# Reciprocal root-mean-square of four head pairs on GpSimd instead of ScalarE, in a fused attention and feed-forward kernel

## Chip, cores and metric

One core of a Trainium2 chip runs the whole kernel. The metric is the device time of one execution in microseconds, given as the median of several runs. A core has a matrix engine (TensorE, PE in the profile), a vector engine (VectorE, DVE), an engine for activation functions (ScalarE, ACT), a general engine (GpSimd, POOL) and a queue that only starts transfers (SyncE, SP). Each engine takes its own instructions strictly in the order in which the program gives them, and waits on semaphores for the results of the others.

## What is computed

The inputs are `q`, `k`, `v` of shape (8, 12, 448, 64): 8 batches, 12 heads, 448 positions, 64 values for each. Cut to what matters:

```python
def rmsnorm(x, g):
    rms = np.sqrt(np.mean(x * x, axis=-1, keepdims=True) + 1e-06)
    return x / rms * g

q_n, k_n = rmsnorm(q, g_q), rmsnorm(k, g_k)
scores = q_n @ k_n.T / sqrt(64)                 # for each batch and head
attn = softmax(scores)
x = (attn @ v).transpose(0, 2, 1, 3).reshape(3584, 768)
out = gelu_tanh(x @ w_in) @ w_out               # w_in 768x2048, w_out 2048x768
```

The change touches only `1 / rms` of the first batch.

## The kernel before

The 12 heads of a batch are worked on as 6 pairs, 0 to 5; a pair fills the 128 partitions with two heads of 64 values. Two pairs make a chunk `c` (pairs 0 and 1, 2 and 3, 4 and 5), and `j` tells which pair of the chunk it is. For batches 1 to 7 the normalization of a batch is done while an earlier batch is in its matrix products. Batch 0 has nothing ahead of it, so its normalization, scores, softmax and products with `v` are woven by hand into a list of steps, `FRONT` (L761 to L774). The function `front` (L669) turns one word of that list into instructions. The order of the words is the order in which each engine gets its work, and nothing reorders it.

The words that matter here, with the pair's number behind them; the letter behind a colon is the engine (A for ScalarE, D for VectorE, P for GpSimd):

- `sq4:P`, `sk4:P`: squares of `q` or `k` of pair 4 (L186 on ScalarE, L188 elsewhere).
- `tq4`, `tk4`: VectorE sums the 64 squares (L203) into `ssq`, 8 columns for `q` and 6 or 8 for `k`.
- `rs4`: `rsqrt` (L205) makes `1 / rms` of both `q` and `k` of the pair, 14 columns for an even pair and 16 for an odd one. ScalarE does it as `Ln` of `ssq / 64 + 1e-6` (L209) and `Exp` of minus one half of that (L212), into the tile `rinv`.
- `nq4:P`, `nk4:P`: `raw * rinv`, to bf16 (L226), on the engine named.
- `tpq4`, `tpk4`: TensorE transposes the result (L238, L245); `cq4`, `ck4`: VectorE copies it from PSUM (L255, L264).
- `s14`: TensorE's scores of one tile of 128 keys for two heads (L324, L310), in one of two PSUM places; `e14`: ScalarE's exponential of that tile (L331), after which the place is free again. There are 21 tiles, seven for each chunk.
- `sa`, `sb`, `xa`, `xb`: the products of a pair with ones, for the sums, and with `v` (L370); `st`, `rc`, `rb`, `xt`: VectorE's reciprocals of the sums, and the scaled result `xT` (L377 to L395).
- `w0` to `w3`, `o0` to `o3`: GpSimd starts the loads of the weights (L630, L636); `v0` to `v2` those of `v`.
- `mb`, `ma`, `mc`, `md`, `g`: the first matrix product of the feed-forward part (L412) and its GELU (L421).

The part of the list around the change:

```
sq0:A sk0:P gcol tq0 tk0 sq1:P rs0 sk1:A nq0:P v1 nk0:D shift tq1 tk1 sq2:A tpq0 tpk0 v2
v0 sk2:A rs1 sq3:A cq0:D ck0:D tq2 s0 e0 y3 s1 nk1:D nq1:D L11 e1 tpk1 tpq1 s2 sk3:P w0
tq3 tk2 rs2 e2 ck1:D cq1:D s3 e3 sa0 s4 sk4:P tk3 nq2:D nk2:D rs3 tpk2 tpq2 s5 sb0 tk4
ck2:D cq2:D nq3:D st0 e4 nk3:P e5 s6 sk5:P L12 e6 tpk3 tpq3 s7 e7 s8 sa1 s9 sb1 xa0 e8
sq4:P sq5:P w1 rc0 cq3:D rb0 ck3:D tq4 tk5 rs4 e9 xb0 s10 st1 xt0 rc1 rb1 tq5 e10 sa2
s11 e11 rs5 nk4:P nq4:P w2 nk5:P nq5:P xa1 xb1 sb2 s12 e12 s13 tpk4 tpq4 xt1 st2 ck4:D
cq4:D rc2 xa2 e13 rb2 sa3 xb2 s14 tpk5 tpq5 s15 e14 xt2 ck5:D cq5:D sb3 e15 U s16 s17
```

Read for one engine, the list gives its queue. GpSimd's from `sk3` on is: `sk3`, `w0`, `sk4`, `nk3`, `sk5`, `sq4`, `sq5`, `w1`, `nk4`, `nq4`, `w2`, `nk5`, `nq5`, `w3`, `o0`, then squares of the next batch.

Of the kernel before, what the change touches and what calls it, by code (L numbers as in the profile page):

```python
# [8 lines left out]
F32 = mybir.dt.float32  # L9
BF16 = mybir.dt.bfloat16  # L10
AF = mybir.ActivationFunctionType  # L11
ALU = mybir.AluOpType  # L12
# [4 lines left out]
def kernel(  # L17
# [11 lines left out]
    nc = tc.nc  # L29
    B, H, S, D = q.shape  # L30
# [19 lines left out]
    consts = ctx.enter_context(tc.tile_pool(name="consts", bufs=1))  # L50
# [11 lines left out]
    op = ctx.enter_context(tc.tile_pool(name="op", bufs=3))  # L62
# [37 lines left out]
    kT = consts.tile([128, NCH, NS, 128], BF16)  # L100

    NU = 4 * CH + 2 * NS
    ssq = [consts.tile([128, NCH, NU], F32, name=f"ss{i}") for i in range(3)]
    raws, sqs, rinvs, nrms = {}, {}, {}, {}
    qT, xT = {}, {}
# [98 lines left out]

    def rsqrt(b, c=slice(0, NCH), at=slice(0, NU)):  # L205
        if b not in rinvs:
            rinvs[b] = smp.tile([128, NCH, NU], F32, tag="rinv", name="rinv")
        lg = smp.tile([128, NCH, NU], F32, tag="lg", name="lg")
        nc.scalar.activation(  # L209
            lg[:, c, at], ssq[b % 3][:, c, at], AF.Ln, scale=1.0 / D, bias=eps  # L210
        )
        nc.scalar.activation(rinvs[b][:, c, at], lg[:, c, at], AF.Exp, scale=-0.5)  # L212
# [397 lines left out]
    nc.vector.memset(ones, 1.0)  # L610
    nc.vector.memset(rows, 1.0)
    nc.vector.memset(ssq[0], 1.0)
    nc.gpsimd.memset(onesr, 0.0)
    for j in range(2):
        nc.gpsimd.memset(onesr[own(j), j], 1.0)
# [53 lines left out]
    def front(step):  # L669
# [7 lines left out]
        elif name in ("tq", "tk"):  # L677
            total(0, c, n, j)
        elif name == "rS":
            rsqrt(0, i, slice(0, 30))  # L680
        elif name == "rs":
            rsqrt(0, c, slice(14 * j, 14 + 16 * j))
        elif name in ("nq", "nk"):
            normed(0, c, n, j, eng)
# [46 lines left out]
        elif name == "o":  # L731
            w_out_part(i // 2, slice(i % 2 * nf // 2, (i % 2 + 1) * nf // 2))
        elif name == "L":
            loads(*divmod(i, 10))
        elif name in ("Sq", "Sk"):
            square(1, i, n, eng)
        elif name in ("Tq", "Tk"):
            total(1, i, n)
        elif name == "Rs":
            rsqrt(1, slice(0, 2))  # L740
        elif name in ("Nq", "Nk"):
            normed(1, i // 10, n, i % 10, eng)
        elif name == "Tp":
            tps["Q", i] = trans(1, i, "q", ps_o, "o")
            tps["K", i] = trans(1, i, "k", ps_m, "mm")
        elif name in ("Cq", "Ck"):
            (place_q if n == "q" else place_k)(1, i, tps[n.upper(), i], eng)
        elif name in ("GELU", "EXP"):
            nc.scalar.preload_act_table_set(EXP_SET if name == "EXP" else GELU_SET)
        elif name == "mb":  # L750
            mm1(0, [0, 1], [i], act=False)
        elif name in ("ma", "mc", "md"):
            fs = [2 * i, 2 * i + 1] if i < 7 else [i + 7]
            cs = {"ma": range(4), "mc": [4], "md": [5] if i < 3 else range(HP)}[name]
            mm1(0, fs, cs, act=False)
        elif name == "g":
            gelu(0, [2 * i, 2 * i + 1] if i < 7 else [i + 7])
        else:
            raise ValueError(step)
# [176 lines left out]
```

## Time and profile before

| | |
|---|---|
| time, median of 3 runs | 413.02 us (412.62 to 413.85) |
| the profiled execution: its time | 413.83 us |
| its span from first to last instruction | 412.1 us |
| busy in the span: TensorE | 403.7 us (98%) |
| VectorE | 274.3 us (67%) |
| ScalarE | 296.2 us (72%) |
| GpSimd | 131.8 us (32%) |

The profile is one execution. All its times count from the start of the span. A row of the timeline gives the start, the duration, the engine, the line, the operation and its tiles; a bracket behind it gives how long the engine had been idle and what ended that. Neighbours of one line are put together with their count. Transposes have the line 238 or 245, and which pair they belong to follows from the order of the list. A row for a stretch gives the busy time of each engine in it and the granted clock of TensorE as a share of full speed. Ends of matrix instructions are modelled, so that busy does not mean working at full rate.

### The profile page before, as it was taken

What the parts mean: (1) busy time and instruction counts of PE and PEld (TensorE: products, weight loads), DVE (VectorE), ACT (ScalarE), POOL (GpSimd) and SP (SyncE); (2) the same over time, 40 slices, a digit from 0 to 9 for tenths busy, and PEclk for the clock granted to TensorE, in tenths of its full rate; (3) what the DMA queues carried; (4) which work ended last, traced back from release to release, by engine and by line L of the source; (5) the groups of instructions that cost most, each with busy time, mean ns of one, the idle gap of its engine ahead of it and who ended that gap; (6) DMA issues with size and microseconds to landing.
All of it is one profiled execution on the core that took longest, in us unless ns stands there. A gap on an engine that the chain in (4) does not pass through costs nothing.

```text
span 412.1 us, 10085 instructions
## 1 busy us (share of the span) xinstructions
PE 403.7 (98%) x4207; PEld 243.5 (59%) x4207; DVE 274.3 (67%) x454; ACT 296.2 (72%) x398; POOL 131.8 (32%) x144
## 2 busy tenths in 40 slices
PE   8799999999999999999999999999999999999996
PEld 3344555566655666557655666556655575556664
DVE  4899739899899638884678747786488633783010
ACT  5797987969988587767977778785976558774300
POOL 7689000234500942037500745019310460000000
PEclk9699999999999999999999999999999999999999
DMA  8999995999981689229981399616991161210022
GB/s 191 227 235 228 203 196 141 227 227 192 213 145 38 139 176 207 66 52 176 222 140 41 78 203 171 136 40 145 171 145 40 23 112 40 72 46 2 2 77 78
DMA packets 97870, 54.21 MB, mean 132 GB/s; under 512 B 63776, under 2 KB 94368, under 8 KB 97824
## 3 DMA queue, kind: packets, MB, share of 16 engines
q1 hardware_dynamic: 71392, 41.69, 43.4%
q0 software_dynamic: 26112, 11.80, 22.5%
q8 instruction: 33, 0.54, 0.6%
q10 hardware_dynamic: 320, 0.07, 0.1%
q14 instruction: 13, 0.11, 0.1%
HBM read 45.61 MB, written 11.01 MB: 137 GB/s over the span
## 4 chain that ended last, share of the span: by engine, by line
PE 95%; SPq 2%; DMA 1%; DVE 0%; ACT 0%; issue 0%; ACTq 0%; DVEq 0%
PE o L441 36%; PE hh L412 31%; PE o L370 11%; PE sc L324 8%; PE h L412 5%; PE sc L310 1%; DMA rawq<-in_q_dram 1%; PE ox L370 1%; SPq L143 1%; SPq L118 1%; SPq L136 1%; PE tp L245 0%; PE o L477 0%; PE tp L238 0%; ACT ex L331 0%
## 5 line engine op out<-in xcount | busy, mean ns | idle before, releaser
L441 PE MATMUL o<-wout,g 128*64 128x384 bf16 (+1 forms) x1648 | 160.6, 327 | 0.0
L331 ACT ACTIVATE ex<-sc,shift 128x896 bf16<-128x896 f32 x144 | 136.1, 1011 | 1.3 <-PE sc L324 1.3
L412 PE MATMUL hh<-xT,win 128*64 128x448 bf16 (+1 forms) x1260 | 133.8, 353 | 0.0
L441 PEld LDWEIGHTS <-g 128*64 128x64 bf16 (+1 forms) x1648 | 96.2, 109 | 58.3 <-issue 14.8
L412 PEld LDWEIGHTS <-win 128*64 128x64 bf16 (+1 forms) x1440 | 95.4, 109 | 49.9 <-issue 3.2
L421 ACT ACTIVATE g<-hh 128x896 bf16<-128x896 f32 x56 | 50.1, 919 | 44.5 <-PE hh L412 44.4
L203 DVE TENSOR_REDUCE ss<-sq 128x14 f32<-128x896 f32 (+4 forms) x45 | 47.9, 1080 | 32.4 <-ACT sq L186 19.9
L454 ACT COPY osb<-o 128x384 f32<-128x384 f32 x50 | 24.2, 483 | 47.8 <-PE o L441 47.8
L788 POOL COPY mark<-es 1x1 bf16<-1x1 bf16 x8 | 1.8, 225 | 162.9 <-DVE es L345 158.5
L377 DVE STREAM_TRANSPOSE st<-o 128x448 f32<-128x448 f32 x48 | 31.1, 648 | 23.6 <-PE o L370 23.2
L324 PE MATMUL sc<-qT,kT 64*128 64x448 bf16 (+1 forms) x372 | 39.6, 360 | 1.7 <-DVE kT L264 1.3
L345 DVE TENSOR_TENSOR es<-ex 128x896 bf16<-128x896 bf16 x42 | 26.8, 637 | 12.0 <-ACT ex L331 12.0
L226 POOL TENSOR_TENSOR nrmq<-rawq,rinv 112x512 bf16<-112x512 f32 x33 | 34.0, 1043 | 0.0
L226 POOL TENSOR_TENSOR nrmk<-rawk,rinv 128x512 bf16<-128x512 f32 (+1 forms) x33 | 31.1, 957 | 4.2 <-ACT rinv L212 4.2
L385 DVE STREAM_TRANSPOSE rb<-rc 128x448 f32<-128x448 f32 x48 | 31.0, 645 | 1.6
L370 PE MATMUL o<-ex,vb 128*64 128x448 bf16 x252 | 30.9, 352 | 0.0
L279 DVE TENSOR_SCALAR kT<-kT,gcol 128x896 bf16<-128x896 bf16 x19 | 21.1, 1108 | 11.7 <-DMA kT<-nrmk 11.7
L343 DVE TENSOR_TENSOR es<-es,exr 64x896 bf16<-64x896 bf16 x42 | 25.9, 617 | 2.4 <-ACT exr L331 1.0
L345 DVE TENSOR_TENSOR es<-es,ex 128x896 bf16<-128x896 bf16 x42 | 25.5, 608 | 2.3 <-ACT ex L331 0.3
L395 DVE TENSOR_TENSOR xT<-o,rb 128x448 bf16<-128x448 f32 x42 | 25.8, 615 | 1.4 <-PE o L370 0.9
L188 POOL TENSOR_TENSOR sq<-rawq 112x1024 f32<-112x1024 f32 x9 | 17.0, 1893 | 28.4 <-DMA rawq<-in_q_dram 25.0
L324 PEld LDWEIGHTS <-kT 64*128 64x128 bf16 (+1 forms) x372 | 10.9, 99 | 24.6 <-issue 18.1
(83 smaller groups left out, 349.4 us busy)
## 6 DMA issues: line engine op xcount, KB each, us to landing
rawq<-in_q_dram SPq DMA_DIRECT2D x48, 224.0 KB, 4.4
rawk<-in_k_dram SPq DMA_DIRECT2D x48, 192.0 KB, 4.6
vb<-in_v_dram POOLq DMA_DIRECT2D x8, 576.0 KB, 10.1
win<-in_moe_w_in_dram POOLq DMA_DIRECT2D x4, 768.0 KB, 14.1
wout<-in_moe_w_out_dram POOLq DMA_DIRECT2D x4, 768.0 KB, 20.4
out_dram<-osb SPq DMA_DIRECT2D x7, 336.0 KB, 4.3
out_dram<-osb SPq DMA_DIRECT2D x8, 288.0 KB, 2.7
out_dram<-osb SPq DMA_DIRECT2D x8, 240.0 KB, 2.6
```

The lines of the kernel that those rows point to most:

```text
L203: nc.vector.reduce_sum(stat(ssq[b % 3], b, c, n, j), view(n, sqs[n, b, c], j), axis=AX.X)
L226: eng.tensor_mul(dst.rearrange("p t a d -> p a t d"), view(n, raws[n, b, c], j), r.to_broadcast(list(r.shape) + [D]),)
L324: nc.tensor.matmul(sc[o, a, :S], kT[r, c, 4 * j + t, o], qT[b][r, hp], start=True, stop=True,)
L331: nc.scalar.activation(dst, sc[:, :, :S], AF.Exp, scale=scale, bias=shift)
L343: nc.vector.tensor_add(es[p], es[p], exrs[b, hp // 2][p])
L345: nc.vector.tensor_add(es, ex[:, 0] if t == 1 else es, ex[:, t])
L370: nc.tensor.matmul(o[a * D:(a + 1) * D], w(a), e[:, a], start=(i == 0), stop=(i + 1 == len(steps)),)
L377: nc.vector.transpose(oas["st"].rearrange("p a b -> p (a b)"), oas[0])
L385: nc.vector.transpose(oas["rb", hp], oas["rc"].to_broadcast([128, S // 32, 32]))
L412: nc.tensor.matmul(h[i * m:(i + 1) * m, j, :S], win[:, c // 2 + NCH * (c % 2), f * 128 + i * m:f * 128 + (i + 1) * m], xT[b][:, c], start= ...
L421: nc.scalar.activation(g[:, fs[0]:fs[0] + len(fs), (b % 2) * S:(b % 2 + 1) * S], hs1[fs[0]][:, :, :S], AF.Gelu_apprx_tanh)
L441: nc.tensor.matmul(o[j * m:(j + 1) * m, :HD], g[:, f, i * 128 + j * m:i * 128 + (j + 1) * m], wout[:, f, half * HD:(half + 1) * HD], start ...
```

## The change

For batch 0 and the chunks 1 and 2, that is in `rs2`, `rs3`, `rs4` and `rs5`, `rsqrt` issues two GpSimd instructions in place of the two ScalarE ones: `ssq / 64 + 1e-6` into `rinv`, then `rinv` to the power of `half`, a constant tile that holds minus one half, in place. `rs0`, `rs1` and all later batches stay on ScalarE. The constant is written by one GpSimd instruction at the start of the program. The list of steps is not changed, so the new instructions stand in GpSimd's queue where the words `rs2` to `rs5` stand in the list: `sk3`, `w0`, `rs2`, `sk4`, `rs3`, `nk3`, `sk5`, `sq4`, `sq5`, `w1`, `rs4`, `rs5`, `nk4`, `nq4`, `w2`, `nk5`, `nq5`.

```diff
     NU = 4 * CH + 2 * NS
+    half = consts.tile([128, NU], F32)
     ssq = [consts.tile([128, NCH, NU], F32, name=f"ss{i}") for i in range(3)]
...
         lg = smp.tile([128, NCH, NU], F32, tag="lg", name="lg")
+        if b == 0 and c > 0:
+            r_ = rinvs[b][:, c, at]
+            nc.gpsimd.tensor_scalar(
+                r_, ssq[b % 3][:, c, at], 1.0 / D, 1e-6, op0=ALU.mult, op1=ALU.add)
+            nc.gpsimd.tensor_tensor(r_, r_, half[:, at], op=ALU.pow)
+            return
         nc.scalar.activation(
             lg[:, c, at], ssq[b % 3][:, c, at], AF.Ln, scale=1.0 / D, bias=eps
         )
...
     nc.vector.memset(ssq[0], 1.0)
+    nc.gpsimd.memset(half, -0.5)
     nc.gpsimd.memset(onesr, 0.0)
```

## The prediction

> **What bounds the kernel now.** I read the span first, then the busy time by stretch, then the chain of waits through the stretch of the change, and last the queues of single engines.
>
> ```profile
> span 412.1 us, 10085 instructions
> ```
>
> The profiled execution took 413.83 us, so 1.7 us lie around its span; it stands 0.81 us above the median of 413.02. I work out a shift D of the end on the rows of this execution and add it to the median.
>
> ```profile
> 10.00:20.00 10.00, 7.31 (x46) 2.85 (x47) 9.21 (x19) 7.82 (x14) 6.43 (x7) 0.70 1.35 227
> 20.00:30.00 10.00, 9.59 (x92) 4.54 (x90) 9.16 (x20) 9.33 (x14) 8.62 (x10) 0.96 1.18 237
> 30.00:36.00 6.00, 6.00 (x50) 2.75 (x51) 5.61 (x10) 5.98 (x7) 5.97 (x5) 1.00 1.19 233
> ```
>
> The columns are the stretch, its length, the busy time of TensorE, its weight loads, VectorE, ScalarE and GpSimd, TensorE's clock, and the transfers. The first batch is the only place where TensorE is not always at work: 2.69 us idle from 10 to 20, 0.41 us from 20 to 30, none from 30 to 36. ScalarE is as full as TensorE from 20 to 36, which makes it tempting to free it.
>
> ```profile
> 13.82 0.53 DVE ss L203
> ...
> 21.09 1.02 ACT ex L331
> 22.10 0.04 issue
> 22.14 0.36 PE sc L324 x2
> ...
> 37.27 0.86 PE hh L412 x4
> ```
>
> This is the chain of waits between 8 and 38 us, 57 pieces. Up to 14.8 it runs through transfers and VectorE, and from there through TensorE, with one visit to ScalarE. Behind 22.14 every piece is TensorE's own. So whatever holds TensorE for a microsecond after 22 us moves the end by a microsecond, unless it saves it elsewhere. What ScalarE costs TensorE in the whole kernel is one row of the waits:
>
> ```profile
> PE sc L324 <- ACT ex L331: 0.4, 1, 0.4
> ```
>
> **What is removed.** Eight ScalarE instructions, four of each kind.
>
> ```profile
> L209 ACT ACTIVATE lg<-ss,eps x7: 292/307/344, 6.0 to 42.3; 128x14 f32<-128x14 f32 x3, 128x16 f32<-128x16 f32 x3, 128x60 f32<-128x60 f32 x1
> L212 ACT ACTIVATE rinv<-lg x7: 214/217/252, 6.4 to 42.7; 128x14 f32<-128x14 f32 x3, 128x16 f32<-128x16 f32 x3, 128x60 f32<-128x60 f32 x1
> ```
>
> By the medians, in ns, that is 4 x (0.307 + 0.217) = 2.1 us of ScalarE. On the path it is worth at most the 0.41 us above.
>
> **What is added.** The constant's write lies in the first 4 us, while GpSimd waits for data: nothing. Each of `rs2` to `rs5` is now two small GpSimd instructions. No row shows a power on GpSimd; the nearest are its multiplications, whose last column is the mean in ns:
>
> ```profile
> L188 POOL TENSOR_TENSOR sq<-rawq 112x1024 f32<-112x1024 f32 x9 | 17.0, 1893 | 28.4 <-DMA rawq<-in_q_dram 25.0 <-DVE ss L203 3.4
> ...
> L188 POOL TENSOR_TENSOR g<-rawk 128x384 f32<-128x384 f32 x2 | 1.7, 834 | 1.0 <-DMA rawk<-in_k_dram 1.0
> ```
>
> The slope is (1893 - 834) / 640 = 1.65 ns a column and the fixed part 0.20 us, so 16 columns multiplied cost 0.22 us. I take that for the first instruction. The power costs at least as much, 0.22 us, and I put its upper end at the longest of these rows, 1.89 us; between them I take the geometric mean, 0.65 us, an estimate, since a power is several multiplications' work on few columns and the fixed part does not grow. With 0.05 us between the two, one `rs` takes 0.92 us (0.49 to 2.16), against 0.55 us on ScalarE.
>
> The Trainium skill ("GPSIMD Engine Reference", section 2.1) says that the first call to a freshly loaded GpSimd kernel pays about 6 us for loading code; if the power were such a call, `rs2` would end 5 us later and I estimate about 421.5. The first multiplications here show nothing of that kind (the 0.84 us of the row at 13.62 below), so the sum leaves it out.
>
> **What is moved.** The order of GpSimd's queue, which is what costs:
>
> ```profile
> 13.62 0.84 POOL L188 TENSOR_TENSOR g<-rawk 128x384 f32<-128x384 f32 x1
> ...
> 23.52 0.82 POOL L226 TENSOR_TENSOR nrmk<-rawk,rinv 128x384 bf16<-128x384 f32 x1 [0.90 <-ACT rinv L212]
> 24.31 1.03 POOL L226 TENSOR_TENSOR nrmq<-rawq,rinv 112x512 bf16<-112x512 f32 x1
> 25.30 0.88 POOL L630 DMA_DIRECT2D win<-in_moe_w_in_dram  x1
> 26.66 1.04 POOL L226 TENSOR_TENSOR nrmk<-rawk,rinv 128x512 bf16<-128x512 f32 x1 [0.47 <-ACT rinv L212]
> 27.66 1.03 POOL L226 TENSOR_TENSOR nrmq<-rawq,rinv 112x512 bf16<-112x512 f32 x1
> ```
>
> These are `sk4`, then `nk4`, `nq4`, `w2`, `nk5`, `nq5`. On ScalarE, `rs5` waited for VectorE's `tq5` and nothing of pair 4 stood behind it. On GpSimd `nk4` and `nq4` do: the list has `rs4`, `rs5`, `nk4`, `nq4`. VectorE's rows:
>
> ```profile
> 11.78 1.53 DVE L226 TENSOR_TENSOR nrmq<-rawq,rinv 112x512 bf16<-112x512 f32 x1
> ...
> 15.57 0.67 DVE L226 TENSOR_TENSOR nrmq<-rawq,rinv 112x512 bf16<-112x512 f32 x1
> 16.17 0.54 DVE L226 TENSOR_TENSOR nrmk<-rawk,rinv 128x384 bf16<-128x384 f32 x1
> ...
> 25.18 0.64 DVE L203 TENSOR_REDUCE ss<-g 112x8 f32<-112x512 f32 x1
> ```
>
> They are `nq1`, `nq2`, `nk2` and `tq5`, which ends at 25.82. And who waits for the normalized pairs, on TensorE:
>
> ```profile
> 16.99 0.50 PE L245 MATMUL tp<-ident,nrmk 128*128 128x128 bf16 x3
> ...
> 26.55 0.34 PE L245 MATMUL tp<-ident,nrmk 128*128 128x128 bf16 x3
> 26.72 0.36 PE L238 MATMUL tp<-ident,nrmq 112*128 112x112 bf16 x4
> ...
> 28.80 0.36 PE L238 MATMUL tp<-ident,nrmq 112*128 112x112 bf16 x4
> ```
>
> These are `tpk2`, `tpk4`, `tpq4` and `tpq5`.
>
> First, **`rs2` and the shared way.** `rs2` starts when `tk2` ends (13.82 + 0.53 = 14.35) and is done at 15.3, ahead of `nq2` at 15.57: no delay by itself. But `sk4` stands behind it and moves from 13.62 to 15.3, so that it lies across `nq2`. Such pairs hold each other up here: `nq1` took 1.53 us against 0.67 for the same work, while GpSimd was squaring. `sk4` would end at 16.15, `nq2` begins 0.6 us late, `nk2` follows, and `rs3` wants its turn between the two. `nk2` then ends near 17.3 instead of 16.71, and `tpk2`, at 16.99 now, starts 0.3 to 0.5 us late. I take u = 0.45 us for the whole first half; with the power at 0.22 us it is about 0.1, with the power at 1.89 us about 2.0 (by the same steps `rs2` ends at 16.5, and `sk4`, `nq2` and `nk2` follow).
>
> Second, **the wait of `rs5`.** `tq5` ends at 25.82 + u, as VectorE's queue in between is full. With 0.08 us for the signal (`nk4` now starts so long after its `rinv`) and `rs5`'s 0.92, `nk4` starts at T = 25.82 + 0.45 + 0.08 + 0.92 = 27.27 instead of 23.52. Behind it, by the starts of the rows, `w2` begins at T + 1.78, `nk5` at T + 2.70, and `nq5` ends 2.03 later, at T + 4.73 = 32.00. `nq4` ends at T + 1.82 = 29.09.
>
> TensorE would reach `tpk4` at 26.55 + u = 27.0 and stands, but for `tpk4` itself, until 29.1; it needs 28.80 - 26.72 = 2.08 us from `tpq4` to `tpq5`, so it reaches that at 31.2 and stands again until 32.04. `tpq5` is late by 32.04 - 28.80 = 3.24 us.
>
> Third, **what comes later.** TensorE has no idle time left to give back. ScalarE runs ahead during the waits and holds nothing up. GpSimd's next squares and weight loads move by the same 3 us as their users, so they add nothing. ScalarE's 0.41 us at 22 us is gained back, but `tq5` does not come earlier for it: VectorE is busy for 9.16 of the 10 us from 20 to 30 (second row of the stretches), and its work up to `tq5` hangs on the transposes of pair 3, not on ScalarE. So D = 3.24 us and the time is 413.02 + 3.24 = **416.3 us**. With the power at 0.22 us T is 26.5 and D 2.4 (415.4); at 1.89 us T is 30.1 and D 6.0 (419.0).
>
> **The rivals.** *The clock falls during the waits.* TensorE's busy time and granted clock in four stretches of 3.4 us:
>
> ```profile
> 7.17:10.59 3.42, 2.26 (x17) 1.00 1.11 231
> 10.59:14.00 3.41, 2.09 (x17) 1.00 1.32 223
> 14.00:17.42 3.42, 2.64 (x17) 0.50 1.49 215
> 17.42:20.83 3.41, 3.41 (x23) 0.50 1.25 244
> ```
>
> A stretch that was 61% busy was followed by half speed for two stretches, one 66% busy was not. My two waits leave 1.24 us idle between 27.66 and 31.07, 64% busy: on the edge. Half speed for one or two stretches costs 1.7 or 3.4 us of work, so 418.0 to 419.7. The Trainium skill ("TensorE: Matmul & The Clock Gate", section "Why this matters for your kernels") asks only that no idle gap be longer than about 3 us; by that rule the clock would hold and 416.3 stand. The trace speaks against the rule, as no gap inside the second stretch can be longer than 3.41 - 2.09 = 1.32 us, and the clock still fell behind it.
>
> *ScalarE sets the pace, and the wait is covered.* This ends on the other side. If TensorE's row of work from 20 to 36 were in truth paced by the exponentials, all 2.1 us would come out: 413.02 - 2.1 = 410.9. For it speaks ScalarE's 5.98 of 6.00 us; against it the chain, with one ScalarE piece of 1.02 us, and the single wait of 0.4 us. It decides if `nk4` starts early enough for `tpq4` at 26.72, that is, by 24.9, before `tq5` has even begun.
>
> *Nothing that can be measured* (413.0): the wait comes, but TensorE makes it up since its rows between 22 and 36 are not at full rate. The chain's unbroken TensorE pieces speak against it.
>
> *The power is far dearer than any row*: at 5 us each, `rs2` alone holds `nq2` for over 4 us, and the end is beyond 421.
>
> **How the numbers follow.** My forecast, the wait of `rs5` at full clock, has 0.57; the same with the clock fallen 0.28; the dear power 0.06; ScalarE's pace 0.05; nothing to measure 0.04. About 0.3%, 1.24 us, is what a measurement of this kernel can tell from no change. The first three are slower (0.91), and the others give 0.05 faster and 0.04 the same. The range goes from 415.0, just under the cheap power, to 420.6, which takes in the fallen clock with a power somewhat dearer than mine; it leaves out the last three cases and the worst of the first two.
>
> **What would show it.** Right: in GpSimd's queue a wait on `ss` of L203 just ahead of the last scaling and power, ending near 26.3; `nk4` near 27.3; on TensorE two idle times, about 2 us ahead of the transposes of pair 4 and 0.8 us ahead of those of pair 5, ended by GpSimd's `nrmq` or `nrmk`; and the end shifted by their sum and u. Power and scaling together are wrong if the two do not take 0.5 to 2.2 us. u is wrong if `tq5` does not end between 25.9 and 26.7. The clock case shows as a granted clock of 0.5 somewhere from 28 to 38 us. The prediction as a whole is wrong if `nk4` starts before 25 us, or if TensorE's idle time before it is not found again at the end.

## The result and the profile after

The changed kernel takes 424.69 us (424.45 to 425.82, 4 runs) against 412.82 for the kernel before (412.42 to 413.85): 11.9 us more, a ratio of 1.0289 (1.0262 to 1.0316). The forecast was 416.3, with a range up to 420.6. It had the direction; the size is outside.

The profiled execution took 424.48 us:

```profile
span 422.7 us, 10087 instructions
```

Here is GpSimd's queue in the timeline of the changed kernel, from `rs2` to `nq5`. The new lines shift the numbers: L212 is the scaling of the sums, L214 the power, L189 the squares, L233 the normalization; further down, on TensorE, L252 are the transposes of `k`, L245 those of `q`, and L419 is the feed-forward part.

```profile
13.57 0.21 POOL L212 TENSOR_SCALAR rinv<-ss 128x14 f32<-128x14 f32 x1
13.86 2.62 POOL L214 TENSOR_TENSOR rinv<-rinv,half 128x14 f32<-128x14 f32 x1
16.47 0.82 POOL L189 TENSOR_TENSOR g<-rawk 128x384 f32<-128x384 f32 x1
17.37 1.00 POOL L212 TENSOR_SCALAR rinv<-ss 128x16 f32<-128x16 f32 x1
18.45 2.91 POOL L214 TENSOR_TENSOR rinv<-rinv,half 128x16 f32<-128x16 f32 x1
21.44 1.55 POOL L233 TENSOR_TENSOR nrmk<-rawk,rinv 128x512 bf16<-128x512 f32 x1
...
27.20 2.61 POOL L214 TENSOR_TENSOR rinv<-rinv,half 128x14 f32<-128x14 f32 x1
30.78 0.20 POOL L212 TENSOR_SCALAR rinv<-ss 128x16 f32<-128x16 f32 x1 [0.97 <-DVE ss L204]
31.07 2.90 POOL L214 TENSOR_TENSOR rinv<-rinv,half 128x16 f32<-128x16 f32 x1
33.94 0.82 POOL L233 TENSOR_TENSOR nrmk<-rawk,rinv 128x384 bf16<-128x384 f32 x1
...
37.66 1.04 POOL L233 TENSOR_TENSOR nrmq<-rawq,rinv 112x512 bf16<-112x512 f32 x1
```

The scaling costs 0.2 us, as assumed, but for the one of 1.00 us at 17.37, which the last section takes up. The power costs 2.6 to 2.9 us, four times the assumed 0.65 and about half as much again as the upper end of 1.89. Between 13.57 and 38.70, where `nq5` ends, GpSimd waits for another engine for 0.97 us in all: the wait of `rs5` is there, at the forecast place, but short, since GpSimd itself comes to it late. TensorE's timeline shows who pays, in the brackets:

```profile
18.36 0.50 PE L252 MATMUL tp<-ident,nrmk 128*128 128x128 bf16 x3 [3.62 <-DVE nrmk L233]
...
23.04 0.61 PE L252 MATMUL tp<-ident,nrmk 128*128 128x128 bf16 x4 [1.94 <-POOL nrmk L233]
...
34.82 0.34 PE L252 MATMUL tp<-ident,nrmk 128*128 128x128 bf16 x3 [3.13 <-POOL nrmk L233]
35.82 0.51 PE L245 MATMUL tp<-ident,nrmq 112*128 112x112 bf16 x4 [0.66 <-POOL nrmq L233]
...
39.43 0.36 PE L245 MATMUL tp<-ident,nrmq 112*128 112x112 bf16 x4
...
44.57 1.69 PE L419 MATMUL hh<-xT,win 128*128 128x448 bf16 x8
```

TensorE waits ahead of the transposes of pairs 2, 3 and 4, one wait for nearly each power, 9.35 us together. `tpq5`, the last row but one, comes at 39.43 instead of 28.80, 10.63 us late; the first matrix product of the feed-forward part (44.57) is late by the same 10.63 (33.94 before), and the span by 10.6. Nothing is given back later.

That the medians differ by 1.3 us more than the spans lies mostly in the execution of before that was profiled: it took 413.83 us, 1.0 above its median. In it `nq1` came just behind `sk3` and took 1.53 us, in the one above it came ahead of it and took 0.69, and the scores of tile 3 began at 13.27 instead of 14.80. The probe below (`e4_probe`), which has the same steps up to the feed-forward part as the kernel before, had `nq1` at 0.68 us and began that part at 33.15; against it the changed kernel is 11.4 us late.

On VectorE the delay is seen at `nq2` and at `tq5`:

```profile
16.52 1.32 DVE L233 TENSOR_TENSOR nrmq<-rawq,rinv 112x512 bf16<-112x512 f32 x1 [2.41 <-POOL rinv L214]
...
30.05 0.64 DVE L204 TENSOR_REDUCE ss<-g 112x8 f32<-112x512 f32 x1
```

`nq2` waits 2.41 us for the power of `rs2` and is then held for 0.6 us more by `sk4`; `tq5` ends at 30.69 instead of 25.82. By stretch, with TensorE first, VectorE third, ScalarE fourth, GpSimd fifth, then TensorE's granted clock:

```profile
10.00:20.00 10.00, 5.22 (x38) 2.32 (x40) 7.12 (x13) 5.65 (x9) 9.07 (x8) 0.77 1.30 222
20.00:30.00 10.00, 8.06 (x48) 2.69 (x46) 5.92 (x12) 5.38 (x6) 9.57 (x8) 0.55 1.17 240
30.00:40.00 10.00, 6.21 (x47) 2.64 (x45) 4.47 (x10) 3.71 (x5) 9.11 (x9) 0.83 0.89 159
```

GpSimd is now the full engine, at over 90% for 30 us, and the other three wait for it. ScalarE, which was to be freed, falls from 9.33 of 10 us to 5.38 between 20 and 30. About 1 us of that are the roots that it no longer computes; for most of the rest it waits for TensorE's scores.

The chain of waits, followed back from the last instruction, does not go through all four powers (the second number is the length of a piece):

```profile
13.86 2.62 POOL rinv L214
...
18.45 2.91 POOL rinv L214
...
21.44 1.55 POOL nrmk L233
...
23.04 0.61 PE tp L252 x4
...
27.14 1.51 PE ox L377 x8
...
30.13 0.58 DVE ss L204
...
31.07 2.90 POOL rinv L214
```

It has the powers of `rs2`, `rs3` and `rs5`. Between the last two lie the transposes of pair 3 and other work of TensorE from 23.04 to 28.65, all at a granted clock of 0.50, and then VectorE up to `tq5`. GpSimd's own row, with the power of `rs4`, is ready for `rs5` only 0.97 us earlier, which is the wait of `rs5`. So the two ways run nearly level, and a faster TensorE could have saved no more than this 0.97 us ahead of `rs5`.

### The profile page after: what moved, and what is told of

It reads as the page before. It is cut to its first block, busy times and chain, and to the rows that moved or that the text cites. A ratio compares the mean times of both kernels' runs of the same rounds, so it can differ in the third digit from the quotient of the medians.

```text
span 422.7 us, 10087 instructions
## 1 busy us (share of the span) xinstructions
PE 406.2 (96%) x4207; PEld 243.6 (58%) x4207; DVE 272.2 (64%) x454; ACT 294.6 (70%) x390; POOL 144.3 (34%) x153
## 4 chain that ended last, share of the span: by engine, by line
PE 92%; POOL 3%; DVE 2%; DMA 1%; issue 0%; ACT 0%; ACTq 0%; POOLq 0%; DVEq 0%
PE o L448 35%; PE hh L419 30%; PE o L377 11%; PE sc L331 8%; PE h L419 4%; POOL rinv L214 2%; PE ox L377 1%; PE sc L317 1%; DMA grow<-in_g_k_dram 1%; DVE ss L204 1%; PE o L484 0%; POOL nrmk L233 0%; PE tp L245 0%; DVE nrmk L233 0%; POOL rinv L212 0%
## 5 line engine op out<-in xcount | busy, mean ns | idle before, releaser
L419 PE MATMUL hh<-xT,win 128*64 128x448 bf16 (+1 forms) x1260 | 133.8, 353 | 0.0
L419 PEld LDWEIGHTS <-win 128*64 128x64 bf16 (+1 forms) x1440 | 95.4, 109 | 49.8 <-issue 3.2
L428 ACT ACTIVATE g<-hh 128x896 bf16<-128x896 f32 x56 | 50.1, 919 | 44.4 <-PE hh L419 44.4
L233 POOL TENSOR_TENSOR nrmq<-rawq,rinv 112x512 bf16<-112x512 f32 x33 | 34.1, 1048 | 0.0
L233 POOL TENSOR_TENSOR nrmk<-rawk,rinv 128x512 bf16<-128x512 f32 (+1 forms) x33 | 31.4, 968 | 0.1
L350 DVE TENSOR_TENSOR es<-es,exr 64x896 bf16<-64x896 bf16 x42 | 25.9, 617 | 2.7 <-ACT exr L338 1.3
L286 DVE TENSOR_SCALAR kT<-kT,gcol 128x896 bf16<-128x896 bf16 x19 | 18.6, 981 | 13.1 <-DMA kT<-nrmk 13.1
L189 POOL TENSOR_TENSOR sq<-rawq 112x1024 f32<-112x1024 f32 x9 | 17.0, 1892 | 27.7 <-DMA rawq<-in_q_dram 24.2
L338 ACT ACTIVATE exr<-sc,shift 128x896 bf16<-128x896 f32 x24 | 24.5, 1019 | 2.3 <-PE sc L317 2.3
```

The source lines that it names most:

```text
L233: eng.tensor_mul(dst.rearrange("p t a d -> p a t d"), view(n, raws[n, b, c], j), r.to_broadcast(list(r.shape) + [D]),)
L338: nc.scalar.activation(dst, sc[:, :, :S], AF.Exp, scale=scale, bias=shift)
L350: nc.vector.tensor_add(es[p], es[p], exrs[b, hp // 2][p])
L419: nc.tensor.matmul(h[i * m:(i + 1) * m, j, :S], win[:, c // 2 + NCH * (c % 2), f * 128 + i * m:f * 128 + (i + 1) * m], xT[b][:, c], start= ...
L428: nc.scalar.activation(g[:, fs[0]:fs[0] + len(fs), (b % 2) * S:(b % 2 + 1) * S], hs1[fs[0]][:, :, :S], AF.Gelu_apprx_tanh)
```

## The experiments

Two theories stood against each other. *Price*: the four powers are long pieces in GpSimd's serial row, and their length is the loss. *Place*: the forecast's main term, `rs5` ahead of pair 4's normalization, is the loss. Besides these, handing work from engine to engine, the clock, and ScalarE's relief were tried.

**A cheap operation in the same place** (`e1_mul`)

```diff
-            nc.gpsimd.tensor_tensor(r_, r_, half[:, at], op=ALU.pow)
+            nc.gpsimd.tensor_tensor(r_, r_, half[:, at], op=ALU.mult)
...
-    nc.gpsimd.memset(half, -0.5)
+    nc.gpsimd.memset(half, 0.9)
```

> The power is replaced by a multiplication with 0.9 in the same four places of GpSimd's queue, so q and k of pairs 2 to 5 of batch 0 are scaled by 0.9 times the mean square; signals, queue and the freed ScalarE stay as in the changed kernel. Theory 'price' (the four powers of 2.6 to 2.9 us are the loss): the multiplication takes about 0.22 us and the prediction's sum for that price holds, 2.4 us over the kernel before, about 415.3. Rival 'handing over' (signals between engines and GpSimd's shared way to the memory are the loss, whatever the operation): stays above 420. Rival 'relief' (ScalarE's 2.1 us would pay if the power were cheap): at or below the kernel before.

415.85 us, 1.0073 (1.0058 to 1.0088): 3.1 us over the kernel before, where the forecast's steps for that price gave 2.4. What is left out here is the root, and with it the right scale of the result; the time alone is of interest. GpSimd's timeline of this kernel has the wait in its forecast form:

```profile
25.32 0.21 POOL L212 TENSOR_SCALAR rinv<-ss 128x16 f32<-128x16 f32 x1 [2.69 <-DVE ss L204]
25.61 0.22 POOL L214 TENSOR_TENSOR rinv<-rinv,half 128x16 f32<-128x16 f32 x1
```

The handing over is not the main loss: signals, queue and the freed ScalarE are all the same here, and 8.8 of the 11.9 us are gone; it lies within the 3.1 that are left. Each power is about 2.54 us longer than the multiplication (2.76 against 0.22), four are 10.2 us, and the wait of `rs5` shrinks by 1.7 us from this kernel to the changed one (2.69 to 0.97): 8.5 us should remain between the two, and 8.8 were measured.

**`nk4` and `nq4` ahead of `rs5`, with the power** (`e2_order`)

```diff
-        s11 e11 rs5 nk4:P nq4:P w2 nk5:P nq5:P xa1 xb1 sb2 s12 e12 s13 tpk4 tpq4 xt1 st2 ck4:D
+        s11 e11 nk4:P nq4:P rs5 w2 nk5:P nq5:P xa1 xb1 sb2 s12 e12 s13 tpk4 tpq4 xt1 st2 ck4:D
```

> The changed kernel with the words nk4 and nq4 ahead of rs5, so that nothing of pair 4 stands behind the wait for tq5. Theory 'price': GpSimd's work is a serial row, nq5 still ends near 37.7 us, so TensorE's transposes of pair 5 come only about 1.7 us earlier: 1.7 us less than the changed kernel. Theory 'place' (the prediction's main term, rs5 ahead of pair 4's normalization, is the loss): 3 us less or more. If neither: no difference.

425.44 us, 1.0294 (1.0267 to 1.0322): no gain at all over the changed kernel, which neither theory had. GpSimd's last row and, from the transposes of pair 5 on, TensorE's, in two fences:

```profile
37.65 1.04 POOL L233 TENSOR_TENSOR nrmq<-rawq,rinv 112x512 bf16<-112x512 f32 x1
```

```profile
37.76 0.61 PE L252 MATMUL tp<-ident,nrmk 128*128 128x128 bf16 x4 [3.30 <-POOL nrmk L233]
38.75 0.55 PE L245 MATMUL tp<-ident,nrmq 112*128 112x112 bf16 x4 [0.39 <-POOL nrmq L233]
...
46.19 1.69 PE L419 MATMUL hh<-xT,win 128*128 128x448 bf16 x8
```

`nq5` ends at 38.69, as in the changed kernel to 0.01 us. In part that is chance, since this execution began `rs2` 0.75 us later, at 14.32; counted from there, GpSimd's row is 24.37 us long against 25.13. So the order saves most of the 0.97 us that GpSimd waited, and no more, because the rest of the row is work. The wait of 3.13 us ahead of pair 4 has gone to pair 5. `tpq5` does come 0.7 us earlier, but from there to the feed-forward part it takes 7.44 us instead of 5.14. TensorE's rows for that time, with its clock behind the busy time, say why:

```profile
38.00:40.00 2.00, 1.61 (x12) 0.50 1.06 154
```

```profile
40.00:42.00 2.00, 2.00 (x14) 0.50 1.22 198
```

Half speed, while the changed kernel has 1.00 from 40 to 42. TensorE has no wait in these 7.44 us, and its clock stays at 0.50 until about 44.4. So the fallen clock cost 2.3 us in the profiled execution, more than `tpq5` had gained.

**The same order with the cheap operation** (`e3_mul_order`; both edits above)

> Multiplication in place of the power as in e1_mul, and nk4 and nq4 ahead of rs5 as in e2_order. By the prediction's own steps pair 4 is ready at 25 us and nq5 ends near 29.3 against 28.8 for tpq5 before: 0.5 us over the kernel before, so about 1.9 us less than e1_mul. Rival (TensorE's wait behind rs5 is covered by something else): no difference from e1_mul. Rival 'relief': below the kernel before by more than 0.4 us.

414.27 us, 1.0035 (1.0021 to 1.0048): 1.6 us less than `e1_mul`, where 1.9 was expected. Where GpSimd has time left, the place of `rs5` costs about what the forecast said. One wait of TensorE for GpSimd is left, 0.43 us ahead of `tpq5`:

```profile
30.06 0.37 PE L245 MATMUL tp<-ident,nrmq 112*128 112x112 bf16 x4 [0.43 <-POOL nrmq L233]
```

**What a power costs** (`e4_probe`: the kernel before, and on GpSimd behind its last weight load)

```diff
+        for n in (1, 4, 8, 14, 16, 30):
+            nc.gpsimd.tensor_tensor(y[:, :n], x[:, :n], e[:, :n], op=ALU.pow)
+        nc.gpsimd.tensor_tensor(y[:16, :16], x[:16, :16], e[:16, :16], op=ALU.pow)
+        nc.gpsimd.tensor_tensor(y[:, :16], x[:, :16], e[:, :16], op=ALU.mult)
+        nc.gpsimd.tensor_scalar(y[:, :16], x[:, :16], 1.0 / D, 1e-6, op0=ALU.mult, op1=ALU.add)
+        nc.gpsimd.memset(e, 1.0)
+        nc.gpsimd.tensor_tensor(y[:, :16], x[:, :16], e[:, :16], op=ALU.pow)
```

> The kernel before, with GpSimd computing on a spare tile while it is otherwise idle behind its last weight load: powers of 1, 4, 8, 14, 16 and 30 columns, one of 16 columns on 16 partitions, a multiplication and a multiply-add of 16 columns, and a power with exponent 1. From the two sizes in the changed kernel (2.61 us for 14 columns, 2.90 for 16): 0.145 us a column and 0.58 us fixed, so 0.73, 1.16, 1.74, 2.61, 2.90 and 4.93 us. Theory 'per column': that line, the same on 16 partitions as on 128. Rival 'per element': the 16-partition one is about an eighth. Rival 'loading code': the first one is several us longer than the line. Rival 'by value': the exponent of 1 costs clearly less. Multiplication and multiply-add 0.2 us. Whole time as before.

The groups by shape; the second number behind the bar is the mean in ns. L120 are the powers, L121 the one on 16 partitions, L125 the one with exponent 1, L122 the multiplication. The one run took 413.28 us, no different from the kernel before, as expected.

```profile
L120 POOL TENSOR_TENSOR osb<-osb 128x30 f32<-128x30 f32 x1 | 5.1, 5124 | 0.1
L120 POOL TENSOR_TENSOR osb<-osb 128x14 f32<-128x14 f32 x1 | 3.2, 3152 | 0.1
L125 POOL TENSOR_TENSOR osb<-osb 128x16 f32<-128x16 f32 x1 | 2.9, 2906 | 0.1
L120 POOL TENSOR_TENSOR osb<-osb 128x16 f32<-128x16 f32 x1 | 2.9, 2899 | 0.1
L121 POOL TENSOR_TENSOR osb<-osb 16x16 f32<-16x16 f32 x1 | 2.9, 2889 | 0.1
L120 POOL TENSOR_TENSOR osb<-osb 128x8 f32<-128x8 f32 x1 | 1.9, 1890 | 0.1
L120 POOL TENSOR_TENSOR osb<-osb 128x4 f32<-128x4 f32 x1 | 1.0, 1024 | 0.1
...
L120 POOL TENSOR_TENSOR osb<-osb 128x1 f32<-128x1 f32 x1 | 0.6, 577 | 0.1
L122 POOL TENSOR_TENSOR osb<-osb 128x16 f32<-128x16 f32 x1 | 0.2, 220 | 0.1
```

From 1 to 30 columns the slope is (5124 - 577) / 29 = 157 ns a column. The power costs by columns, the same on 16 partitions as on 128, and the same for an exponent of 1. The theory "per column" holds, but two rows lie above a straight line through the others: 8 columns by about 0.2 us and 14 by over 0.5 (3.15 us here, 2.62 in the kernel). The multiply-add missed its 0.2 us too, with 0.61. All three began while VectorE was in an instruction with two inputs in SBUF (its normalizations from 42.22 to 45.68, and a sum of tiles from 58.97 to 59.59), which the last section comes back to; that this is their whole cause was not tested. The first power, one column, took 0.58 us, and the first in the changed kernel, 0.08 us behind its scaling, took 2.62, as long as the third, which has the same size. So no loading of code shows. The 6 us that the Trainium skill names for the first call to a freshly loaded kernel ("GPSIMD Engine Reference", section 2.1) do not occur here.

**No root at all** (`e5_free`)

```diff
+            if b == 0:
+                nc.vector.memset(rinvs[b][:, 1:], 0.9)
...
-            nc.gpsimd.tensor_scalar(
-                r_, ssq[b % 3][:, c, at], 1.0 / D, 1e-6, op0=ALU.mult, op1=ALU.add)
-            nc.gpsimd.tensor_tensor(r_, r_, half[:, at], op=ALU.pow)
             return
```

> rs2 to rs5 are left out on every engine: pairs 2 to 5 of batch 0 are scaled by the constant 0.9, which VectorE writes once, so neither ScalarE's eight instructions nor any wait for a reciprocal root is left. This bounds what taking the roots off ScalarE can bring at best. Theory 'TensorE and the order of the pairs set the pace' (the prediction): the one wait of 0.4 us for ScalarE goes, 0.3 to 0.6 us less than the kernel before, at 412.3. Rival 'relief' (ScalarE sets the pace from 20 to 36 us): 2.1 us less, at 410.7.

413.58 us, 1.0017 (1.0005 to 1.0030). Not even the 0.3 to 0.6 us came. TensorE's timeline, from the scores of tile 3 (L315) to the feed-forward part (L417 here):

```profile
13.11 0.88 PE L315 MATMUL sc<-qT,kT 64*64 64x448 bf16 x4 [0.76 <-DVE kT L269]
...
20.38 0.36 PE L329 MATMUL sc<-qT,kT 64*128 64x448 bf16 x2 [0.39 <-ACT ex L336]
...
32.58 1.69 PE L417 MATMUL hh<-xT,win 128*128 128x448 bf16 x8
```

From the one to the other it takes 19.47 us, against 19.14 in the kernel before, though ScalarE has eight instructions less and nobody waits for a root; the wait of 0.4 us for ScalarE is still there. ScalarE's relief is worth nothing here, so with this order of the list no way of doing the roots elsewhere can be expected to win. What makes this version slightly slower was not pursued.

**TensorE's clock kept up** (`e6_warm`)

```diff
-        tq3 tk2 rs2 e2 ck1:D cq1:D s3 e3 sa0 s4 sk4:P tk3 nq2:D nk2:D rs3 tpk2 tpq2 s5 sb0 tk4
+        tq3 tk2 rs2 e2 ck1:D cq1:D s3 e3 sa0 s4 sk4:P tk3 nq2:D nk2:D rs3 y34 tpk2 tpq2 s5 sb0 tk4
-        ck2:D cq2:D nq3:D st0 e4 nk3:P e5 s6 sk5:P L12 e6 tpk3 tpq3 s7 e7 s8 sa1 s9 sb1 xa0 e8
+        ck2:D cq2:D nq3:D st0 e4 nk3:P e5 s6 sk5:P L12 e6 y18 tpk3 tpq3 s7 e7 s8 sa1 s9 sb1 xa0 e8
```

> The changed kernel with empty matrix products in TensorE's waits ahead of the transposes of pair 2 (34 of 224 columns, about 3.3 us) and of pair 3 (18, about 1.7 us), so that its clock stays up from 15 to 29 us. Theory 'price': the row of GpSimd sets the end; a faster TensorE brings tq5 forward, so that rs5 follows rs4 at once (0.97 us of waiting goes), 1 us less than the changed kernel. Theory 'clock' (half speed over those 13.7 us is most of what the sum of powers does not explain): 3 us less or more. If the clock costs nothing: no difference.

424.69 us, 1.0281 (1.0264 to 1.0297), no different from the changed kernel. The words `y34` and `y18` are 34 and 18 empty products. The clock did stay up, though only from about 20 to 33 us; TensorE's row from 22 to 24 has 1.00 where the changed kernel has 0.50, and GpSimd's `nq5` still ends where it did:

```profile
22.00:24.00 2.00, 2.00 (x21) 1.00 1.16 219
```

```profile
37.45 1.05 POOL L233 TENSOR_TENSOR nrmq<-rawq,rinv 112x512 bf16<-112x512 f32 x1
```

TensorE is faster and only waits longer, 3.82 us ahead of pair 4. `rs5` does follow `rs4` at once, as "price" said, and counted from `rs2` GpSimd's row is 24.27 us long instead of 25.13. But this execution began `rs2` 0.66 us later than the changed kernel's (14.23), and the clock fell again between 33 and 34 us, so that TensorE came to `tpq5` 0.87 us after the end of `nq5`; the expected 1 us did not show in the time. What a full clock behind pair 4 would be worth in the changed kernel was not tested. There `tpq5` begins 0.73 us after `nq5` ends, so by that row it is at most about 0.7 us; with the 0.97 us of `rs5` the fallen clock has at most about 1.7 of the 11.9 us, an estimate from these two rows.

**Half the change each** (`e7_first` and `e8_last`)

```diff
-        if b == 0 and c > 0:
+        if b == 0 and c == 1:     # e7_first: rs2, rs3
+        if b == 0 and c == 2:     # e8_last: rs4, rs5
```

> Only rs2 and rs3 on GpSimd, rs4 and rs5 on ScalarE as before. Theory 'price': the two powers stand in GpSimd's queue ahead of sk4, nk3, sk5, sq4 and sq5, so the whole front is shifted by about their length, 4 to 6 us over the kernel before. Theory 'place': rs5's wait is gone, at most 1 us over.

> Only rs4 and rs5 on GpSimd, rs2 and rs3 on ScalarE as before. By the prediction's steps with the measured prices: tq5 at 25.8, rs4 done at 25.6, rs5 at 29.0, nq5 at 33.8 against 28.8 for tpq5: 5 us over the kernel before. Theory 'price': this and e7_first add up to the whole loss, 11.9 us, within 1.5 us. Theory 'place': this alone has nearly the whole loss, 9 us or more.

419.41 us, 1.0157 (1.0143 to 1.0170), and 419.17 us, 1.0151 (1.0136 to 1.0166), against 412.81: 6.6 and 6.4 us, together 13.0, or 1.1 more than the whole change. Two powers cost half of what four do, wherever they stand; the place of `rs5`, which only the second has, does not set it apart, where "place" wanted at most 1 us for the one and 9 or more for the other. Both are more than was expected (4 to 6 us, and 5). TensorE's clock was at 0.50 in parts of both, but what the excess is was not tested.

**TensorE's clock kept up in the kernel before** (`e11_warm_before`, `e12_warm_more`). After the run with the other order the clock looked like something to be won without the change, so empty products went into TensorE's early waits with the roots on ScalarE.

```diff
-        v0 sk2:A rs1 sq3:A cq0:D ck0:D tq2 s0 e0 y3 s1 nk1:D nq1:D L11 e1 tpk1 tpq1 s2 sk3:P w0
-        tq3 tk2 rs2 e2 ck1:D cq1:D s3 e3 sa0 s4 sk4:P tk3 nq2:D nk2:D rs3 tpk2 tpq2 s5 sb0 tk4
+        v0 sk2:A rs1 sq3:A cq0:D ck0:D tq2 s0 e0 y3 s1 nk1:D nq1:D L11 e1 tpk1 y9 tpq1 s2 sk3:P w0
+        tq3 tk2 rs2 e2 ck1:D cq1:D y8 s3 e3 sa0 s4 sk4:P tk3 nq2:D nk2:D rs3 tpk2 tpq2 s5 sb0 tk4
```

`e12_warm_more` has `y13` ahead of `s0` besides.

> The kernel before, roots on ScalarE, with empty matrix products in two of TensorE's early waits: 9 of 224 columns ahead of the transposes of q of pair 1 (1.05 us idle) and 8 ahead of the scores of tile 3 (0.78 us idle). Theory 'clock': the stretch from 10.6 to 14.0 us is then over 85% busy, the half speed from 14.0 to 20.8 us does not come, and of some 6 us of work at half speed up to 3 us are gained: 410 to 411.5. Rival 'price/others set the pace' (what holds the front is VectorE and GpSimd, as in the run with fillers in the changed kernel): within 0.3% of the kernel before. Rival: the clock still falls, since empty products count too little: as before.

> As e11_warm_before, and 13 more empty products ahead of the scores of tile 0 (1.30 us idle). Theory 'clock': as e11_warm_before or up to 0.5 us better, since two stretches are now busy. Rival 'others set the pace': within 0.3% of the kernel before. If the empty products delay real ones: up to 0.5 us more than e11_warm_before.

412.63 us (11 runs) against 413.14, 0.9996 (0.9976 to 1.0016); and 413.31 us, 1.0014 (0.9993 to 1.0035). In `e11_warm_before` the clock stayed up where it had been 0.50:

```profile
16.00:18.00 2.00, 1.94 (x20) 1.00 1.37 227
```

Yet no gain can be told from none, with runs from 411.99 to 416.68. The single profiled execution was 1.8 us shorter in span (410.3) than that of the kernel before, which was itself 1.0 us above its median; this decides nothing. `e12_warm_more` brought nothing further. Whether the half speed at the start costs the kernel before anything stays open; what these empty products can gain is below 0.3%.

## Why the prediction was wrong in its size

*What bounds the kernel, and what ScalarE's relief is worth*: right. TensorE gave nothing back, the shift at `tpq5` reached the end whole, and with all roots left out nothing was gained (`e5_free`).

*The price of the power*: this is the step that failed. The sum put in 0.65 us, and it is 2.6 to 2.9 (`e4_probe`: 157 ns a column, against 1.65 for a multiplication, some 95 times as much). The longest GpSimd row was to be the upper end. But that row is long because it has 1024 columns of cheap work; it bounds nothing about another operation. Hence the upper end, and with it the range, was too low. The forecast's own line, carried on to 2.76 us, gives a loss of 7.9 us, about 420.9. So the price explains 4.6 of the 8.4 us by which the forecast fell short; the other 3.8 are in the next step. The case of a power dearer than any row was named, with a chance of only 0.06. The row at 13.62, which was to speak against a loading of code, is neither a power nor GpSimd's first multiplication (that one is at 4.37, 0.83 us); the first power of the probe settles it.

*How the price turns into time*: half right. At the cheap end the steps were tested by themselves: 2.4 us forecast, 3.1 measured (`e1_mul`), and the part of it that lies in the order, 1.9 against 1.6 (`e3_mul_order`). Above that the forecast's line was too flat. From 0.22 to 1.89 us it rose by 3.6 us, 2.2 for each microsecond of the power; between `e1_mul` and the changed kernel it is 8.8 / 2.54 = 3.5. With the power at 0.22 us GpSimd has 2.69 us to spare ahead of `rs5`, and this soaks up what comes earlier; in the changed kernel only 0.97 us of it is left.

The profiled shift can be put into the forecast's terms. It came out at 10.63 us instead of 3.24, and 4.4 of these 7.4 us are u, the delay of the first half: 0.45 us forecast, while `tq5` came 4.87 us late (it ended at 30.69, where the forecast called u wrong outside 25.9 to 26.7). `rs2` and `rs3` do this alone (in `e7_first` `tq5` ends at 30.61, against 30.69). Another 2.2 us are `rs5` itself, 0.92 forecast and 3.16 from its start to `nk4`. The last 0.7 are TensorE, which at half speed comes to `tpq5` 0.73 us after `nq5` is done, where the forecast had 0.04. From `nk4` to `nq5` the forecast was right, 4.76 us against 4.73. Part of u is the clock: from the transposes of pair 3 to the end of `tq5` it takes 7.65 us, most of it at 0.50, and 5.66 in `e6_warm` at 1.00, but there the power of `rs4` holds `rs5` up in its place.

*The wait of `rs5`*: right as a mechanism, and shown in `e1_mul` and `e3_mul_order`, but not what the changed kernel loses most of its time to. There it is 0.97 us, and taking it away brought no gain in the time (`e2_order`), though there the clock fell as well. That the forecast had the direction owes something to this wait, but the size of the loss comes from the powers. Of the two idle times that it named on TensorE, the one ahead of pair 4 came (3.13 and 0.66 us); the one ahead of pair 5 did not.

*The clock*: it fell, as the rival said, but was not the main cause. With the clock up from 20 to 33 us the time was the same (`e6_warm`), and by the estimate above it has at most about 1.7 of the 11.9 us. It matters behind the last wait on GpSimd, as the 2.3 us of `e2_order` show.

## What to carry to other kernels

An operation that no row of the trace shows can't be bounded by rows of another operation, however long they are; measure it once by itself, in a stretch where its engine is idle, and look at what the other engines do there: three rows of the probe above came out too long. An engine at a third of its time over the whole span can be nearly full in the stretch that counts: look at its waits there, and at how much new work fits into them before every further microsecond reaches the end. And before work is moved off an engine, leave it out once: if that gains nothing, as here, no other place for it is likely to.

## What the runs showed of the hardware

The cost of a power on GpSimd goes by the columns of the tile and not by its elements: 2.89 us for 16 columns on 16 partitions, 2.90 on 128. For 14 values in each of 128 rows it is five times ScalarE's two instructions together (2.62 us against 0.30 + 0.22).

GpSimd and VectorE hold each other up even in the smallest instructions: the scaling for `rs3` took 1.00 us in place of 0.21, while VectorE's `nq2`, itself held up by `sk4`, was running and, right behind it, `nk2` (17.76 to 18.31); it ended at 18.37 (GpSimd's row at 17.37, VectorE's at 16.52). The Trainium skill ("SBUF — State Buffer", section "Who interferes with whom") says that a VectorE instruction with two inputs in SBUF and a GpSimd instruction that reads SBUF exclude each other, and the rows agree. A long power did not do the same to VectorE: in `e4_probe` a normalization that lay within the power of 16 columns took 0.68 us (at 49.42), as long as `nk1` at 11.18 in the kernel before; this is one case.
